# A third matmul on 128 rows instead of 64 in the up-projection of a fused attention, FFT-mixing and token-mixing kernel

## The chip, the cores and the metric

The kernel runs on 1 core of one Trainium2 chip. The metric is the device time of the whole program in microseconds, from the first to the last instruction with the launch around it, as the median of several runs. One more execution was taken with the hardware profiler; all rows of the trace come from that execution.

## What is computed

Three layers follow each other on a tensor of 4 batches, 4224 tokens and 192 features. The first is a convolution over the last 7 tokens with weights from a softmax. The second adds the real part of a two-dimensional FFT, normalizes, and applies a two-layer MLP of width 768. The third rotates by learned angles, mixes the tokens with two 4224x4224 matrices, and applies one more small dense layer. In the second layer, which the change touches:

```python
mixed = np.real(X).astype(np.float32)          # X: fft over tokens, then features
u = x + mixed
un = (u - mu) / np.sqrt(var + 1e-06)
ch = np.maximum(un @ w_ch1, 0.0) @ w_ch2       # 192 -> 768 -> 192
return (u + ch).astype(np.float32)
```

The token mixing of the third layer is `yr + yi`, with `yr = w_tok_r @ zr` and `yi = w_tok_i @ zi`; it holds by far the most arithmetic.

## The kernel before

**Precision.** TensorE is fed 32-bit words in its `F32R` form. Where more precision is wanted, an operand is split into a high part, which `F32R` holds exactly, and a low part, the rest. A product is then high x high + low x high + high x low. The weights arrive as 64-bit words, and `convert` (line 346) makes float32 of them from the bytes, on ScalarE and VectorE, and splits them into high and low parts. This byte-wise conversion is in the kernel before and after and is not touched.

**Two stages.** The prologue does the convolution and the FFT. `main_phase` then runs everything else in one interleaved program whose order is written out by hand as a list of steps: each step `t` of the last loop issues half of a slot of the token mixing, and whatever pieces of other work are due at that step.

**Token mixing.** It is cut into 33 blocks of 128 source tokens and 12 chunks of 352 target tokens. A unit is one block and one chunk; its weights are loaded by SyncE (703.6 KB each, 396 of them), converted some steps ahead (`CONV_STEPS`) into a tile `ws`, and multiplied on line 844: 128 rows, 352 columns, three products of parts. In the paired phases a slot is 12 matmuls into one PSUM tile of the pool `ps_y` (3 buffers); VectorE adds the result to `acc` (line 431).

**Preparation.** The inputs of the mixing, `z`, are made in 66 preparations `prep(k)`, one for each token block and pair of batches, on 256 columns (two batches of 128 tokens). From the fourth on, a preparation begins every `PAIR_STEPS` = 36 steps; the first four (k = 0, 2, 1, 3, in `BEGIN`) begin before the mixing does. In a preparation, step 7 transposes the normalized rows, steps 8 and 9 split them into `uT`; steps 13 to 31 (`MLP_STEPS`) hold the MLP in six pieces of 128 hidden features, each of which is `up(ft)` (five matmuls into a PSUM tile `psh`, lines 537 to 541), `act(ft)` (Relu on ScalarE at line 549, its low part on VectorE at line 550) and `down(ft)` (four matmuls, lines 563 and 564). The rest of the preparation makes the angles, sine and cosine and the products `z`, the last of them on GpSimd (line 674).

**The layout around the change.** The 192 input features are held as 128 + 64. `uT[:, 0]` is the high part of the first 128 features and `uT[:, 2]` their low part. `uT[:, 1]` holds the last 64 features twice: rows 0 to 63 are the high part (line 521), rows 64 to 127 the low part (line 526). The weights `w1s` lie in four slots, the high parts in 0 and 1, the low parts in 2 and 3; slots 1 and 3 hold the rows of the last 64 features twice, in rows 0 to 63 and again in rows 64 to 127. So the fourth matmul (slot 1 against `uT[:, 1]`, 128 rows) gives high x high and high x low at once, and the third (slot 3 against `uT[:, 1]`, 64 rows) gives low x high.

The page names a group of instructions by its line. A matmul of a shape `64*128 64x256` uses 64 rows and 128 columns of the array and moves 256 columns through it.

Of the kernel before, what the change touches and what calls it, by code (L numbers as in the profile page):

```python
# [379 lines left out]
def main_phase(tc, I, xs, mx, out, state):  # L380
    nc = tc.nc
    with ExitStack() as ctx:
# [14 lines left out]
        w1s = wt.tile([P, 4, DFF], F32R, name="w1s")  # L397
# [65 lines left out]
        def prep(k):  # L463
# [67 lines left out]
            def up(ft):  # L531
                def go():
                    uT = v["uT"]
                    c = slice(ft * P, ft * P + P)
                    ps = hs[ft] = ps_h.tile([P, 2 * P], F32, tag="h", name=f"psh{k}{ft}")
                    mm = nc.tensor.matmul
                    mm(ps, w1s[:, 0, c], uT[:, 0], start=True, stop=False)  # L537
                    mm(ps, w1s[:, 2, c], uT[:, 0], start=False, stop=False)  # L538
                    mm(ps, w1s[:64, 3, c], uT[:64, 1], start=False, stop=False)  # L539
                    mm(ps, w1s[:, 1, c], uT[:, 1], start=False, stop=False)  # L540
                    mm(ps, w1s[:, 0, c], uT[:, 2], start=False, stop=True)  # L541

                return go
# [24 lines left out]
            for ft in range(6):  # L568
                a, b, c = MLP_STEPS[ft]
# [125 lines left out]
        for i in range(HEAD):  # L695
            c, n = slots[3 * i][1], slots[3 * i][3]
# [34 lines left out]
        start = {}  # L731
# [80 lines left out]
        for t in range(T0, 2 * len(slots) + 24):  # L812
# [21 lines left out]
            js, c, m, n0 = slots[t // 2]  # L834
            pr, mo = divmod(m, 3)
            parts_n = 2 * len(js)
            if t % 2 == 0:
                ps = ps_y.tile([P, 1, TCH], F32, tag="y", name=f"y{t}")
# [127 lines left out]
```

## Time and profile before

| What | Value |
|---|---|
| Median of 3 runs | 3552.22 us (3549.4 to 3553.26) |
| The profiled execution: its time | 3549.07 us |
| The profiled execution: its span | 3547.4 us |
| TensorE matmul busy (PE) | 3397.7 us, 96% of the span, 20980 instructions |
| TensorE weight load busy (PEld) | 3248.7 us, 92% |
| VectorE busy (DVE) | 2408.4 us, 68% |
| ScalarE busy (ACT) | 2108.3 us, 59% |
| GpSimd busy (POOL) | 743.8 us, 21% |
| Mean DMA rate | 109 GB/s |

PE is the array at work on matmuls and PEld its loading of the stationary operand, which may overlap. The matmuls are pipelined, so the durations of neighbours overlap too; the distance from one start to the next is what a matmul costs in a dense stream. An arrow `<-` names what ended a wait.

### The profile page before, as it was taken

Reading aid. Unit: us, or ns where it says so; the run is one execution under the profiler, and the core shown is the slowest. Engines: PE = TensorE matmul, PEld = TensorE weight load, DVE = VectorE, ACT = ScalarE, POOL = GpSimd, SP = SyncE. Lnnn points to the kernel's source line nnn. Section 1 sums busy time; section 2 is a strip of 40 time slices with the busy share of each in tenths; the row PEclk is TensorE's granted clock in tenths of the full one; section 3 lists DMA queues with packets and bytes.
Section 4 is the critical chain, followed back from the end, with each engine's and each line's share of the span. In section 5 each row is a group of like instructions: output and inputs, shape, how many; then the busy total and the mean of one; then the engine's idle time right before and its main releaser. Section 6 shows DMA issues by size and latency. Waiting matters only on the chain.

```text
span 3547.4 us, 54487 instructions
## 1 busy us (share of the span) xinstructions
PE 3397.7 (96%) x20980; PEld 3248.7 (92%) x20980; DVE 2408.4 (68%) x5351; ACT 2108.3 (59%) x3280; POOL 743.8 (21%) x672
## 2 busy tenths in 40 slices
PE   4778799999999999999999999999999999999999
PEld 3667689999999999999999999999999999999999
DVE  8998566666666666666666666666666666666666
ACT  1333656666666666666666666666666666666643
POOL 8997111111111111111111111111111111111133
PEclk8889899999999999999999999999999999999999
DMA  4464123332323233232333323333333333333333
GB/s 158 164 207 136 60 91 100 106 105 101 108 99 107 97 105 107 99 107 99 107 101 105 108 99 107 100 106 100 103 107 100 107 100 107 104 102 107 108 121 117
DMA packets 119668, 388.03 MB, mean 109 GB/s; under 512 B 10096, under 2 KB 64112, under 8 KB 118768
## 3 DMA queue, kind: packets, MB, share of 16 engines
q1 hardware_dynamic: 116672, 376.62, 31.7%
q10 hardware_dynamic: 2736, 7.94, 0.6%
q8 instruction: 164, 2.69, 0.3%
q14 instruction: 96, 0.79, 0.1%
HBM read 351.88 MB, written 32.64 MB: 108 GB/s over the span
## 4 chain that ended last, share of the span: by engine, by line
PE 85%; ACT 1%; DVE 1%; POOL 0%; issue 0%; DMA 0%; POOLq 0%; ACTq 0%; DVEq 0%
PE y L844 63%; PE ch L563 4%; PE psh L540 3%; PE psh L539 3%; PE fy L787 2%; PE ch L564 2%; PE psh L537 1%; PE psh L541 1%; PE psh L538 1%; PE pst L621 1%; PE pst L609 1%; PE psu L513 1%; PE psx L593 0%; ACT cq L360 0%; DVE f L369 0%; ACT cq L361 0%
## 5 line engine op out<-in xcount | busy, mean ns | idle before, releaser
L844 PE MATMUL y<-ws,z 128*128 128x352 f32 x14256 | 2483.7, 325 | 7.2 <-DVE acc L433 4.4
L844 PEld LDWEIGHTS y<-ws,z 128*128 128x128 f32 x14256 | 2277.7, 189 | 9.2 <-DVE acc L433 4.9
L431 DVE TENSOR_TENSOR acc<-y,acc 128x352 f32<-128x352 f32 (+1 forms) x1158 | 597.7, 516 | 239.3 <-PE y L844 231.4
L374 ACT CAST ws<-f 128x704 fp32r<-128x704 f32 x396 | 309.1, 781 | 424.3 <-DVE f L369 424.3
L360 ACT ACTIVATE cq<-cq,bounds 128x704 uint8<-128x704 uint8 x396 | 347.6, 878 | 162.3 <-DVE cq L357 162.0
L363 DVE SCALAR_TENSOR_TENSOR cq<-cx,cq 128x176 int32<-128x176 int32 x396 | 135.5, 342 | 446.7 <-ACT cq L361 446.2
L663 POOL TENSOR_TENSOR r<-r,x 128x256 f32<-128x256 f32 (+1 forms) x260 | 188.0, 754 | 1167.7 <-ACT r L656 1167.7
L367 ACT ACTIVATE f<-cq 128x704 int32<-128x704 int8 x396 | 312.9, 790 | 135.9 <-DVE cq L363 135.8
L369 DVE SCALAR_TENSOR_TENSOR f<-raw,f 128x704 int32<-128x704 int32 x396 | 355.2, 897 | 33.8 <-ACT f L367 33.5
L376 DVE TENSOR_TENSOR ws<-f,ws 128x704 fp32r<-128x704 f32 x396 | 352.1, 889 | 30.8 <-ACT ws L374 30.6
L361 ACT ACTIVATE cq<-cq,bounds 128x704 uint8<-128x704 uint8 x396 | 349.4, 882 | 13.0
L550 DVE SCALAR_TENSOR_TENSOR g<-psh,g 128x256 fp32r<-128x256 f32 x384 | 162.0, 422 | 258.7 <-ACT g L549 258.4
L355 ACT COPY cx<-raw 128x704 uint8<-128x704 uint8 x396 | 326.1, 823 | 0.0
L496 POOL TENSOR_SCALAR rs<-mv 128x2 f32<-128x2 f32 x66 | 13.2, 200 | 1330.3 <-DVE mv L495 1301.4
L563 PE MATMUL ch<-w2s,g 128*128 128x384 f32 x768 | 241.5, 351 | 2.6 <-DVE spare L579 1.3
L549 ACT ACTIVATE g<-psh 128x256 fp32r<-128x256 f32 x384 | 144.0, 375 | 121.4 <-PE psh L541 121.4
L564 PE MATMUL ch<-w2s,g 128*128 128x192 f32 x768 | 194.1, 253 | 0.6 <-DVE g L550 0.5
L674 POOL TENSOR_TENSOR z<-r,z 128x768 fp32r<-128x768 f32 x66 | 121.9, 1847 | 135.1 <-ACT z L669 135.1
L564 PEld LDWEIGHTS ch<-w2s,g 128*128 128x128 f32 x768 | 146.7, 191 | 2.2 <-DVE g L550 2.2
L563 PEld LDWEIGHTS ch<-w2s,g 128*128 128x128 f32 x768 | 144.9, 189 | 4.1 <-ACT g L549 2.5
L149 POOL TENSOR_TENSOR pa<-pa,pb 128x768 f32<-128x768 f32 (+1 forms) x76 | 147.2, 1937 | 5.9
L540 PE MATMUL psh<-uT,w1s 128*128 128x256 f32 x384 | 148.3, 386 | 0.0
(172 smaller groups left out, 3830.3 us busy)
## 6 DMA issues: line engine op xcount, KB each, us to landing
raw<-in_W SPq DMA_DIRECT2D x396, 703.6 KB
xin<-in_xa SPq DMA_DIRECT2D x28, 960.0 KB
out<-fo SPq DMA_DIRECT2D x24, 528.0 KB
mx<-mxd SPq DMA_DIRECT2D x63, 192.0 KB
xs<-xn SPq DMA_DIRECT2D x28, 384.0 KB
mxd<-mxt SPq DMA_DIRECT2D x4, 1632.0 KB
xin<-in_xa SPq DMA_DIRECT2D x4, 1056.0 KB
wraw<-in_wts ACTq DMA_DIRECT2D x1, 3263.6 KB
```

The costliest lines, as they stand in the source:

```text
L355: nc.scalar.copy(x.bitcast(U8), tops)
L360: nc.scalar.activation(q8, q8, AF.Relu, bias=bounds[:, 0:1], scale=-1.0)
L361: nc.scalar.activation(q8, q8, AF.Relu, bias=bounds[:, 1:2], scale=-8.0)
L367: nc.scalar.activation(ti, q.bitcast(I8), AF.Copy, scale=2.0**24)
L369: nc.vector.scalar_tensor_tensor(ti, words, 5, ti, op0=ALU.logical_shift_right, op1=ALU.bitwise_or)
L374: nc.scalar.copy(h, t)
L376: nc.vector.tensor_tensor(out=l(), in0=t, in1=h.bitcast(F32), op=ALU.subtract)
L431: nc.vector.tensor_tensor(out=d, in0=v, in1=d, op=ALU.add)
L540: mm(ps, w1s[:, 1, c], uT[:, 1], start=False, stop=False)
L563: nc.tensor.matmul(ch[:, i, 0 : 2 * D], g[:, 0, t], w, start=ft == 0, stop=False)
L564: nc.tensor.matmul(ch[:, i, D : 2 * D], g[:, 1, t], w[:, :D], start=False, stop=ft == 5)
L844: nc.tensor.matmul(ps[:, 0], zz[hl], s[:, hw, ri], start=q + n == 0, stop=q == parts_n - 1 and n == 2)
```

## The change

The third of the five matmuls of `up` takes all 128 rows of its two operands instead of the first 64. Its upper 64 rows add low x low, the product of the low parts of the last 64 features, which the kernel before leaves out. The number of instructions stays, and nothing else is touched.

```diff
                     mm(ps, w1s[:, 0, c], uT[:, 0], start=True, stop=False)
                     mm(ps, w1s[:, 2, c], uT[:, 0], start=False, stop=False)
-                    mm(ps, w1s[:64, 3, c], uT[:64, 1], start=False, stop=False)
+                    mm(ps, w1s[:, 3, c], uT[:, 1], start=False, stop=False)
                     mm(ps, w1s[:, 1, c], uT[:, 1], start=False, stop=False)
                     mm(ps, w1s[:, 0, c], uT[:, 2], start=False, stop=True)
```

## Rows read from the trace of the kernel before

**Rows 1.** Busy time by stage: us, busy of PE, PEld, DVE, ACT, POOL, granted clock, DMA.
```profile
core 0: us, PE busy (x) PEld busy (x) DVE busy (x) ACT busy (x) POOL busy (x), PEclk, DMA share, GB/s
400.00:462.00 62.00, 46.29 (x253) 38.50 (x253) 37.58 (x88) 32.34 (x58) 13.65 (x19) 0.86 0.16 54
...
1000.00:2000.00 1000.00, 1000.00 (x6223) 964.15 (x6223) 656.84 (x1466) 640.55 (x959) 123.86 (x154) 1.00 0.31 104
```

**Rows 2.** Chain of work that ended last, 520 to 3320 us: shares, two pieces.
```profile
by line: PE y L844 75.8%; PE ch L563 4.8%; PE psh L540 4.1%; PE psh L539 4.1%; PE ch L564 2.3%; PE psh L537 1.5%; PE psh L541 1.5%; PE psh L538 1.5%; PE pst L621 1.4%; PE pst L609 1.2%; PE psu L513 1.0%; PE psx L593 0.5%; PE psx L594 0.2%
...
570.91 6.72 PE y L844 x42
616.87 6.72 PE y L844 x42
```

**Rows 3.** PE groups by shape, 520 to 3320 us: busy us, mean ns, idle before.
```profile
L540 PE MATMUL psh<-uT,w1s 128*128 128x256 f32 x366 | 140.7, 384 | 0.0
L539 PE MATMUL psh<-uT,w1s 64*128 64x256 f32 x366 | 139.7, 382 | 0.0
...
L537 PE MATMUL psh<-uT,w1s 128*128 128x256 f32 x366 | 102.7, 281 | 0.0
```

**Rows 4.** PE in order of time, one up piece: start us, us, instruction.
```profile
1507.00 0.28 PE L537 MATMUL psh<-uT,w1s 128*128 128x256 f32 x1
1507.12 0.28 PE L538 MATMUL psh<-uT,w1s 128*128 128x256 f32 x1
1507.33 0.38 PE L539 MATMUL psh<-uT,w1s 64*128 64x256 f32 x1
1507.64 0.38 PE L540 MATMUL psh<-uT,w1s 128*128 128x256 f32 x1
1507.86 0.28 PE L541 MATMUL psh<-uT,w1s 128*128 128x256 f32 x1
1507.98 2.09 PE L844 MATMUL y<-ws,z 128*128 128x352 f32 x12
```

**Rows 5.** Line 539 in three stretches: count, ns min/median/max, first and last start.
```profile
L539 PE MATMUL psh<-uT,w1s x12: 379/380/580, 379.0 to 419.5; 64*128 64x256 f32 x12
...
L539 PE MATMUL psh<-spare,w1s x12: 379/382/384, 394.8 to 458.2; 64*128 64x256 f32 x12
...
L539 PE MATMUL psh<-uT,w1s x6: 380/382/382, 495.7 to 513.9; 64*128 64x256 f32 x6
...
L539 PE MATMUL psh<-uT,w1s x366: 380/382/383, 539.3 to 3317.5; 64*128 64x256 f32 x183
```

**Rows 6.** Chain of work, 370 to 540 us: the last VectorE piece, first up piece.
```profile
499.88 0.35 DVE g L550
500.27 0.36 PE ch L564
...
501.42 0.12 PE psh L537
501.54 0.12 PE psh L538
```

**Rows 7.** PE's waits, 378 to 462 us: us in total, times, longest us.
```profile
PE psu L513 <- DVE spare L503: 10.0, 1, 10.0
```

**Rows 8.** PE in order of time at the lower clock, one up piece.
```profile
382.34 0.47 PE L537 MATMUL psh<-uT,w1s 128*128 128x256 f32 x1
...
383.85 0.42 PE L541 MATMUL psh<-uT,w1s 128*128 128x256 f32 x1
384.06 0.52 PE L563 MATMUL ch<-w2s,g 128*128 128x384 f32 x1
```

**Rows 9.** VectorE and PE in order of time around one MLP piece.
```profile
1501.45 0.42 DVE L527 TENSOR_TENSOR uT<-psu,uT 128x256 fp32r<-128x256 f32 x1
...
1508.10 0.42 DVE L550 SCALAR_TENSOR_TENSOR g<-psh,g 128x256 fp32r<-128x256 f32 x1
...
1510.08 0.25 PE L564 MATMUL ch<-w2s,g 128*128 128x192 f32 x1
```

## The prediction, made before the changed kernel was run

> **What bounds the kernel now.** I read the busy times by stage first. From 520 to 3320 us TensorE is busy for all of every stage; the row of 1000 to 2000 us stands for them, with PE at 1000.00 of 1000 us, VectorE at 656.84, ScalarE at 640.55, and a granted clock of 1.00, which is the upper of the two levels, 2.4 GHz [rows 1]. Busy is not the same as well used, so the next view is the chain of work that ended last. In that stretch it consists of TensorE's lines alone, no other engine stands in it, and it repeats: the run of 42 mixing matmuls begins at 570.91 and again at 616.87, so one preparation takes 45.96 us [rows 2]. The groups by shape say the same: no idle time before any of them [rows 3]. So a nanosecond taken from TensorE's stream in this stretch is a nanosecond off the end, until another engine is late.
>
> The same chain shows the odd thing. The five matmuls of an up piece are alike but for one's row count, yet lines 537, 538 and 541 take 1.5% of the stretch each, and 539 and 540 take 4.1% each [rows 2]. Line 539 is the one on 64 rows; 540 follows it and has the full 128 rows, as 537 has, but its mean is 384 ns against 281 [rows 3].
>
> **What the change removes.** Starts in order of time give the cost [rows 4]: from 537 to 538 it is 0.12 us, then 0.21 to 539, 0.31 to 540, 0.22 to 541, and 0.12 to the next mixing matmul. Together the piece takes 1507.98 - 1507.00 = 0.98 us. Two plain steps of this shape are 0.12 each at the precision of the rows. The shares give a third figure: 1.5% of 2800 us over 366 pieces is 0.115 us. I take 0.117 us. Five of these are 0.585, so the piece has 0.98 - 0.585 = 0.39 us that its columns don't explain: 0.09 before the 64-row matmul starts, 0.19 between it and its follower, 0.10 after the follower. All of it lies around the passage from 128 rows to 64 and back: the weight load for the next shape isn't hidden behind the matmul of the last one. The shares check the sum: (4.1 - 1.5) x 2 = 5.2% of 2800 us is 146 us over 366 pieces, 0.40 each.
>
> With the change all five have one shape, 128 rows and 256 columns, the shape of 537 and 538. The third's own streaming costs nothing more for its rows if the 0.12 us of 537, with 128 rows, holds for it too; the trace has no plain 64-row stream beside it in this stage, so I bound that step below by 0.115 and above by 0.21, its present distance, and take 0.117, since the shape after the change is exactly that of 537.
>
> The Trainium skill has a rule that speaks against a gain: "TensorE: Matmul & The Clock Gate", in "Why this matters for your kernels", says that a matmul on 32 contraction rows takes the same time as one on 128. By it alone the third matmul costs the same on 64 rows as on 128 and nothing is won, which is a rival below; the rows of lines 539 and 537, 382 against 281 ns on equal columns, disagree with it for a 64-row matmul in this place [rows 3]. "TensorEngine Tiling (Array Packing)", under "Key Properties", says that a change of the tiling mode drains the engine. By that both passages of each piece cost time and both go, and the sum stays what the rows give.
>
> **How often, and where.** There are 396 pieces, 66 preparations of six [rows 5]. 366 lie from 539.3 to 3317.5 us, wholly in TensorE's stretch. The six of the fifth preparation start their third matmul between 495.7 and 513.9; the chain passes from VectorE to TensorE at 500.27 and holds the up piece at 501.42 [rows 6], so four of these count. That makes 370 x 0.39 = 144 us.
>
> The other 26, from 379.0 to about 500 us, lie where the clock is granted at 0.86 on average and PE is busy 46.29 of 62 us [rows 1], and where TensorE waits 10.0 us at one point for VectorE's work on the normalized rows [rows 7]. If that wait swallows all, they give nothing; if all is passed on they give 26 x 0.39 = 10 us, plus about one for the few pieces at the lower clock. I take 4, under the middle, as the long wait lies behind most of them.
>
> **What it adds.** No instruction, no DMA, no semaphore of a new kind; the queues of SyncE and GpSimd are passed by nothing. The third matmul now also reads rows 64 to 127 of `uT[:, 1]`, which line 526 on VectorE writes just ahead of 527. The fourth read them already, 0.31 us later. In the preparation of the rows, 527 ends at 1501.87 and a first up piece starts at about 1504, some 2 us later [rows 9], so the earlier read waits for nothing; without that cover it could cost at most those 0.31 us in one piece of six, some 20 us in all. The upper rows of the weight slot are filled long before, by the same conversion as the lower.
>
> **What is late next.** A preparation shrinks by 6 x 0.39 = 2.36 to 43.6 us. VectorE's 656.84 us in 1000 are 30.2 us of 45.96, or 69% of 43.6, and ScalarE's 640.55 become 68%, so neither is the bound on the mean [rows 1]. In the dense part of the MLP, VectorE's low part (line 550) ends at 1508.52 and its reader on TensorE starts at 1510.08, a cover of 1.56 us [rows 9]. Two up pieces lie ahead of that reader and bring it 0.78 us nearer; half of the cover stays. Behind 550 on VectorE's queue is the next addition to `acc`, which frees one of three `y` buffers. If each preparation lost another 0.5 us there, it would be 30 us.
>
> **The sum.** The profiled execution took 3549.07 us, a span of 3547.4 and 1.7 around it, 3.15 us below the median of the runs. 3549.07 - 144 - 4 = 3401; on the median, 3552.22 - 148 = 3404 us.
>
> **The rivals.**
> - *Only half of the passage goes.* If the delay after the fourth matmul (0.10 us to 541) belongs to its operands and not to the row change, 370 x 0.10 = 37 us stay: 3441 us. For it: the fourth and the third share `uT[:, 1]`. Against: 541 after 540 has the shapes of 538 after 537, which start 0.12 us apart [rows 4].
> - *Another engine takes the bound in the MLP part*, VectorE through its low parts and `acc`. With the 0.5 us above: 3434 us; at 1 us, 3465. Against it stand the 69% and the cover that is left.
> - *No gain*, the rule of the skill: the distances belong to the third and fourth place in the sum, or row count costs nothing either way: 3552 us. Against it stand 539 and 540 beside 537 [rows 3].
> - *Slower: the clock.* The array works on more rows, and the lower clock level is granted during the up pieces. At the lower level a plain step was 0.21 us (383.85 to 384.06) and a whole piece before the change 1.72 [rows 8]. A changed piece would take 5 x 0.21 = 1.05 us against 0.98 now, +0.07: 370 times that is +26 us, 3578 us. It decides from the point where over 0.39 / (1.05 - 0.585), some 84%, of the pieces run at the lower level. Against it: four of the five matmuls and all of the mixing have 128 rows already, at a granted clock of 1.00 [rows 1, 4].
>
> That the change doesn't do what it says would be this: the compiled instruction keeps 64 rows. Its price is that of no gain, and it is in that chance.
>
> **How the numbers follow.** Full gain 0.85; half of the passage 0.04; another engine late 0.06; no gain 0.03; slower 0.02. The forecast's own bounds are 3392 (all 26 early pieces pass on their 11 us, and a few us of spread between runs) and 3412 (none do, and the piece falls short by some 0.01 us). Toward the other cases I reach to 3425, part of the way to a late VectorE. A difference of 0.2%, about 7 us, is what a measurement of this kernel can tell from none. Faster by more than that: 0.95; within it 0.03; slower 0.02.
>
> **What would show it.** In the profile after, lines 537 to 541 should each be 128*128 with about 281 ns, start 0.12 us apart, with the piece at 0.59 us; the pieces of the chain repeat every 43.6 us; the shares of 539 and 540 fall to about 1.6%; PE stays without idle time from 520 us on, and the end moves by what PE's stream lost. A later start of 541 alone would be the first rival; idle time before 564 or 844 with VectorE as its releaser the second. The forecast is wrong if line 539 on 128 rows still starts 0.2 us after 538.

## The result, and the profile after

| | Before | After |
|---|---|---|
| Median of 4 runs | 3552.74 us | 3408.51 us (3405.7 to 3410.29) |
| Ratio to before | | 0.9601, 95% interval 0.959 to 0.9613 |
| Profiled execution: time (span) | 3549.07 us (3547.4) | 3409.65 us (3407.9) |

The medians lie 144.2 us apart, the two profiled executions 139.4. The forecast was 148 us less, 3404 us, with 3392 to 3425 as its range.

The first view of the kernel after is its busy time by stage, with the columns of [rows 1]. TensorE still has no free moment in the steady stretch, at the same granted clock of 1.00; VectorE's share grew from 656.84 to 690.14 us in 1000 because the same work is done in less time.

```profile
1000.00:2000.00 1000.00, 1000.00 (x6550) 998.64 (x6550) 690.14 (x1548) 672.59 (x1009) 130.25 (x161) 1.00 0.33 109
```

The chain of work of the kernel after, from 520 to 3180 us, answers to [rows 2]. Lines 539 and 540 fell from 4.1% to 1.6%, the share that 537, 538 and 541 have too. The run of 42 mixing matmuls comes back after 611.23 - 567.55 = 43.68 us, where it was 45.96.

```profile
by line: PE y L844 79.8%; PE ch L563 5.1%; PE ch L564 2.5%; PE psh L540 1.6%; PE psh L539 1.6%; PE psh L541 1.6%; PE psh L537 1.6%; PE psh L538 1.6%; PE pst L621 1.5%; PE pst L609 1.2%; PE psu L513 1.0%; PE psx L593 0.5%; PE psx L594 0.3%
...
567.55 6.72 PE y L844 x42
611.23 6.72 PE y L844 x42
```

The groups by shape from 520 to 3180 us answer to [rows 3]: the third matmul now shows 128 rows, and its mean and the fourth's, which the change doesn't touch, are within 3 ns of the first's.

```profile
L539 PE MATMUL psh<-uT,w1s 128*128 128x256 f32 x366 | 103.5, 283 | 0.0
L540 PE MATMUL psh<-uT,w1s 128*128 128x256 f32 x366 | 103.5, 283 | 0.0
...
L537 PE MATMUL psh<-uT,w1s 128*128 128x256 f32 x366 | 102.7, 280 | 0.0
```

In order of time, one piece of the same preparation as in [rows 4] and [rows 9], with the low part on VectorE and its reader:

```profile
1457.66 0.28 PE L537 MATMUL psh<-uT,w1s 128*128 128x256 f32 x1
...
1457.78 0.28 PE L538 MATMUL psh<-uT,w1s 128*128 128x256 f32 x1
...
1457.90 0.28 PE L539 MATMUL psh<-uT,w1s 128*128 128x256 f32 x1
...
1458.02 0.28 PE L540 MATMUL psh<-uT,w1s 128*128 128x256 f32 x1
...
1458.14 0.28 PE L541 MATMUL psh<-uT,w1s 128*128 128x256 f32 x1
...
1458.26 2.09 PE L844 MATMUL y<-ws,z 128*128 128x352 f32 x12
...
1459.17 0.42 DVE L550 SCALAR_TENSOR_TENSOR g<-psh,g 128x256 fp32r<-128x256 f32 x1
...
1460.19 0.19 PEld L564 LDWEIGHTS ch<-w2s,g 128*128 128x128 f32 x1
1460.37 0.25 PE L564 MATMUL ch<-w2s,g 128*128 128x192 f32 x1
```

All starts are 0.12 us apart, and the piece takes 1458.26 - 1457.66 = 0.60 us instead of 0.98. VectorE's result is ready at 1459.59 and read at 1460.37: the cover went from 1.56 to 0.78 us, and TensorE shows no wait in the steady stretch. The low part is the stationary operand there, so it is the weight load of line 564 that needs it, and that starts earlier than its matmul: at 1509.91 before and 1460.19 after. Counted to the load, the cover went from 1.39 to 0.60 us. The load before:

```profile
1509.91 0.19 PEld L564 LDWEIGHTS ch<-w2s,g 128*128 128x128 f32 x1
```

### The profile page after: what moved, and what is told of

Read it like the earlier page. It is cut to its first block, busy times and chain, and to the rows that moved or that the text cites. A ratio compares the mean times of both kernels' runs of the same rounds, so it can differ in the third digit from the quotient of the medians.

```text
span 3407.9 us, 54487 instructions
## 1 busy us (share of the span) xinstructions
PE 3249.6 (95%) x20980; PEld 3201.5 (94%) x20980; DVE 2404.2 (71%) x5351; ACT 2103.6 (62%) x3280; POOL 744.3 (22%) x672
## 4 chain that ended last, share of the span: by engine, by line
PE 84%; ACT 1%; DVE 1%; POOL 0%; issue 0%; DMA 0%; POOLq 0%; ACTq 0%; DVEq 0%
PE y L844 66%; PE ch L563 4%; PE fy L787 2%; PE ch L564 2%; PE psh L540 1%; PE psh L539 1%; PE psh L541 1%; PE psh L537 1%; PE psh L538 1%; PE pst L621 1%; PE pst L609 1%; PE psu L513 1%; PE psx L593 0%; ACT cq L360 0%; DVE f L369 0%; ACT cq L361 0%
## 5 line engine op out<-in xcount | busy, mean ns | idle before, releaser
L145 POOL TENSOR_TENSOR pb<-xin,w 128x768 f32<-128x768 f32 (+1 forms) x76 | 123.2, 1620 | 0.0
```

## The experiments

The theory under test: a passage of the array from 128 rows to 64 and a passage back cost about 0.2 us each, whatever the matmul reads and wherever it stands. Its rivals: the delay belongs to the third and fourth matmul and their shared operand; each 64-row matmul is slow in itself; every departure from the neighbours' shape costs.

Each was run in rounds with the kernel before on the same chip. A first set compares with 3550.89 us before, a second with 3549.24.

**The 64 rows moved to another matmul.** The change, with the fifth on 64 rows:

```diff
-                    mm(ps, w1s[:, 0, c], uT[:, 2], start=False, stop=True)
+                    mm(ps, w1s[:64, 0, c], uT[:64, 2], start=False, stop=True)
```

> The changed kernel with its fifth matmul on 64 rows (the upper 64 rows of that product are left out); the third stays on 128. Passage theory: any 64-row matmul between 128-row ones costs one passage to 64 rows and one back, wherever it stands and whatever it reads, so the 0.385 us a piece come back: 3408.5 + 370 x 0.385 = 3551 us, with the late starts now at 541 and at the mixing matmul behind it. Operand theory: the delay belonged to the third and fourth, which share uT[:, 1]; the fifth reads another tile part, so 3408 us.

It took 3548.59 us, 0.9995 of before (0.9985 to 1.0005): the whole gain is gone again. Its PE in order of time:

```profile
1507.35 0.28 PE L540 MATMUL psh<-uT,w1s 128*128 128x256 f32 x1
1507.56 0.38 PE L541 MATMUL psh<-uT,w1s 64*128 64x256 f32 x1
1507.87 0.43 PE L844 MATMUL y<-ws,z 128*128 128x352 f32 x1
```

The steps of 0.21 and 0.31 us moved along, to the fifth and to the mixing matmul behind it, which has another operand, another shape and another PSUM tile. The operand theory falls. The forecast's first rival, a delay of the fourth's own operands, falls with it.

**96 rows.** The kernel before, with

```diff
-                    mm(ps, w1s[:64, 3, c], uT[:64, 1], start=False, stop=False)
+                    mm(ps, w1s[:96, 3, c], uT[:96, 1], start=False, stop=False)
```

> The kernel before with its third matmul on 96 rows instead of 64 (32 of the low x low rows are in). If only the passage to the 64-row setting of the array costs, 96 rows run in the 128-row setting and the time is that of the change, 3408 us, with 540 starting 0.12 us after 539. If any row count other than that of the neighbours costs, 3552 us.

It took 3407.74 us, 0.96 of before (0.9585 to 0.9614), the time of the change. Its PE in order of time:

```profile
1502.32 0.28 PE L539 MATMUL psh<-uT,w1s 96*128 96x256 f32 x1
1502.44 0.28 PE L540 MATMUL psh<-uT,w1s 128*128 128x256 f32 x1
```

So it isn't a row count other than the neighbours' that costs: 96 rows run among 128 at 0.12 us a step.

**32 rows.** The same line with `w1s[:32, 3, c], uT[:32, 1]`.

> The kernel before with its third matmul on 32 rows instead of 64 (the other 32 rows of that product are left out). Passage theory: a 32-row setting is another division of the array, and there and back cost the same, 3551 us. If the delay goes by the number of rows (fewer to load and to fill), 3480 us or another time clear of 3551.

3551.61 us, 1.0006 of before (0.9997 to 1.0015). The steps are those of 64 rows, though half as many rows are loaded and multiplied:

```profile
1508.13 0.38 PE L539 MATMUL psh<-uT,w1s 32*128 32x256 f32 x1
1508.44 0.39 PE L540 MATMUL psh<-uT,w1s 128*128 128x256 f32 x1
1508.66 0.28 PE L541 MATMUL psh<-uT,w1s 128*128 128x256 f32 x1
```

**64 columns instead of 64 rows.** The changed kernel, with

```diff
-                    mm(ps, w1s[:, 3, c], uT[:, 1], start=False, stop=False)
+                    mm(ps[:64], w1s[:, 3, ft * P : ft * P + 64], uT[:, 1], start=False, stop=False)
```

> The changed kernel with its third matmul on 128 rows but only 64 stationary columns (the third product is left out for half of the hidden features). If every change in how the array is divided costs a passage, columns as well as rows, 3551 us. If only the rows matter, 3408 us or a little less.

3401.59 us, 0.9582 of before (0.9568 to 0.9596). No passage is seen on either side:

```profile
1509.47 0.28 PE L538 MATMUL psh<-uT,w1s 128*128 128x256 f32 x1
1509.59 0.28 PE L539 MATMUL psh<-uT,w1s 128*64 128x256 f32 x1
1509.71 0.28 PE L540 MATMUL psh<-uT,w1s 128*128 128x256 f32 x1
```

By the medians, this kernel took 6.9 us less than the change. Its third weight load takes 135 ns instead of 188, and its steady stretch, from the first to the last start of line 539, is 3170.4 - 535.7 = 2634.7 us against 2639.6 after the change; how the one leads to the other wasn't tried.

**Two 64-row matmuls, apart and together.** The first kernel is the one before, with its fifth matmul on 64 rows as well, so that the 128-row fourth stands between two of 64:

> The kernel before with a second 64-row matmul, the fifth, so that third and fifth stand on 64 rows with the 128-row fourth between them (the upper 64 rows of the fifth's product are left out). Two passages there and two back in each piece. Passage theory: 3551 + 370 x 0.385 = 3693 us. If the later matmuls hide part of a second passage, between 3600 and 3693. If what costs is one fixed pause per piece: 3551 us.

The second puts the same fifth ahead of the fourth, so that the two of 64 rows are neighbours:

```diff
-                    mm(ps, w1s[:, 1, c], uT[:, 1], start=False, stop=False)
-                    mm(ps, w1s[:, 0, c], uT[:, 2], start=False, stop=True)
+                    mm(ps, w1s[:64, 0, c], uT[:64, 2], start=False, stop=False)
+                    mm(ps, w1s[:, 1, c], uT[:, 1], start=False, stop=True)
```

> The same two 64-row matmuls as in the run with two passages there and back, but next to each other: the fifth's product goes ahead of the fourth's (the same 64 rows of one product are left out). One passage there and one back. Passage theory: 3551 us, as with one 64-row matmul, and the second 64-row matmul starts about 0.12 us after the first. If each 64-row matmul is itself slow, 3551 + 370 x 0.19 to 370 x 0.385 = 3621 to 3693 us.

Apart they took 3706.14 us, 1.0441 of before (1.0425 to 1.0457); together 3550.65 us, 1.0004 (0.9995 to 1.0013). The same five matmuls, in another order, differ by 155 us. So a 64-row matmul isn't slow in itself, and the passages are what is paid for. The chains of the two, in the same view as above, give the price: a preparation takes 48.32 us apart and 45.98 together.

```profile
731.24 6.72 PE y L844 x42
779.56 6.72 PE y L844 x42
```
```profile
709.50 6.72 PE y L844 x42
755.48 6.72 PE y L844 x42
```

Against the 45.96 us of before, the second pair of passages costs (48.32 - 45.96) / 6 = 0.39 us a piece, as much as the first. The time missed the theory's 3693 us by 13, and that lies ahead of the steady stretch. The third matmul starts first at 378.7 us and opens the steady stretch at 552.3, where before it was 379.0 and 539.3 [rows 5]; from 378 to 420 us the granted clock was 0.59, between its two levels, against 0.88 before. The theory's 370 pieces left 26 early ones out. The stage before, and with the two 64-row matmuls apart (columns as in [rows 1]):

```profile
378.00:420.00 42.00, 38.71 (x193) 30.36 (x192) 24.12 (x74) 20.49 (x54) 5.86 (x9) 0.88 0.26 88
```
```profile
378.00:420.00 42.00, 41.94 (x137) 31.35 (x135) 18.57 (x59) 13.16 (x39) 1.77 (x4) 0.59 0.24 82
```

One part of what I expected of the neighbours was a miss: the second was to start 0.12 us after the first, and it took 0.22:

```profile
1505.26 0.28 PE L538 MATMUL psh<-uT,w1s 128*128 128x256 f32 x1
1505.47 0.39 PE L539 MATMUL psh<-uT,w1s 64*128 64x256 f32 x1
1505.69 0.28 PE L540 MATMUL psh<-uT,w1s 64*128 64x256 f32 x1
1505.90 0.39 PE L541 MATMUL psh<-uT,w1s 128*128 128x256 f32 x1
1506.12 0.33 PE L844 MATMUL y<-ws,z 128*128 128x352 f32 x1
```

The piece still takes 1506.12 - 1505.14 = 0.98 us; its first matmul starts at 1505.14. The rows read best so: a passage delays two starts in a row, the one that passes by about 0.09 us and the next by about 0.10. Here the four late starts stand apart, at 0.21 to 0.22 each. In the kernel before, the second delay of the way down and the first of the way back fall on the same matmul, which makes its 0.31 [rows 4].

The weight loads say more of it. First those of the kernel before, in the piece of [rows 4], then those of the two neighbours:

```profile
1507.00 0.19 PEld L538 LDWEIGHTS psh<-uT,w1s 128*128 128x128 f32 x1
1507.33 0.18 PEld L539 LDWEIGHTS psh<-uT,w1s 64*128 64x128 f32 x1
1507.64 0.19 PEld L540 LDWEIGHTS psh<-uT,w1s 128*128 128x128 f32 x1
1507.75 0.19 PEld L541 LDWEIGHTS psh<-uT,w1s 128*128 128x128 f32 x1
```
```profile
1505.47 0.18 PEld L539 LDWEIGHTS psh<-uT,w1s 64*128 64x128 f32 x1
1505.58 0.19 PEld L540 LDWEIGHTS psh<-uT,w1s 64*128 64x128 f32 x1
1505.90 0.19 PEld L541 LDWEIGHTS psh<-uT,w1s 128*128 128x128 f32 x1
```

Without a passage, a load starts some 0.11 us ahead of its matmul, while the one before still runs: line 538's at 1507.00 for 1507.12, and the neighbour's at 1505.58 for 1505.69. Across a passage it starts only with its own matmul, at 1507.33 and 1507.64, and at 1505.47 and 1505.90. In the steady stretch of every kernel here with a 64- or 32-row matmul, the third to fifth matmul's loads that cross a passage start 0 to 3 ns ahead of their matmuls, and the others 113 ns or more. With 96 rows, with 64 columns and after the change, all five have that lead.

**No third matmul.** The changed kernel with line 539 taken out:

> The changed kernel without its third matmul (low x high of the last 64 features is left out). If the third costs one plain step of 0.119 us and TensorE stays the bound, 3408.5 - 370 x 0.119 = 3364 us, and the fourth starts 0.12 us after the second. If VectorE is about to be late behind the shorter MLP part, less is won and idle time stands before 564 or 844 in the steady stretch: 3380 to 3408 us.

3364.03 us, 0.9475 of before (0.9461 to 0.9489), 44.5 us below the change: 0.12 us for each of 370. So a 128-row step of 256 columns costs its 0.12 us and no more, and the 64-row form had cost 0.12 + 0.39. VectorE is hardly late even now: between 520 and 3100 us, TensorE's only wait in this kernel is one of half a microsecond, for VectorE:

```profile
PE psx L592 <- DVE x L578: 0.5, 1, 0.5
```

**The first four preparations alone.** The kernel before, with

```diff
-                    mm(ps, w1s[:64, 3, c], uT[:64, 1], start=False, stop=False)
+                    r3 = P if k in BEGIN else 64
+                    mm(ps, w1s[:r3, 3, c], uT[:r3, 1], start=False, stop=False)
```

> The change in the first four preparations alone (24 pieces, from 379 to about 460 us), the other 62 as before. My forecast took 4 us for the early pieces, 0 to 11 as bounds: 3547 us. If the waits of that stretch swallow the gain, as the profile after suggests (the steady stretch began only about 1 us earlier): 3550 to 3551 us.

3547.43 us, 0.9993 of before (0.9984 to 1.0001): by the time alone, the 4 us and no gain can't be told apart. The trace tells more. The rows are the third matmul (here on line 540), with counts and first and last start as in [rows 5]; first this kernel, then the changed one:

```profile
L540 PE MATMUL psh<-uT,w1s x12: 278/281/415, 378.8 to 416.3; 128*128 128x256 f32 x12
...
L540 PE MATMUL psh<-uT,w1s x6: 380/382/383, 492.2 to 510.6; 64*128 64x256 f32 x6
```
```profile
L539 PE MATMUL psh<-uT,w1s x12: 278/280/415, 382.5 to 420.0; 128*128 128x256 f32 x12
...
L539 PE MATMUL psh<-uT,w1s x6: 282/282/283, 495.4 to 513.1; 128*128 128x256 f32 x6
```

From the first third matmul of all to the first of the fifth preparation it is 495.7 - 379.0 = 116.7 us before [rows 5], 492.2 - 378.8 = 113.4 here and 495.4 - 382.5 = 112.9 after the change. The early stretch became 3.3 and 3.8 us shorter. This isn't shown to be the passages alone, because the granted clock changed with them: from 378 to 420 us it was 0.88 before and 0.96 in both of these kernels. The kernel with 32 rows, which has as many passages as before, was granted 0.72 there and took 499.0 - 378.5 = 120.5 us. In the profiled execution after the change this can't be seen from the steady stretch alone, because there the stretch ahead of the pieces, in which nothing was changed, ended 3.5 us later than in that of before.

## Why the prediction was right

- **The bound.** TensorE alone sets the end from 520 us on: held. Its stream lost 3317.5 - 539.3 - (3177.7 - 538.1) = 138.6 us in the steady stretch, from the first and last start of line 539 in [rows 5] and after (538.1 to 3177.7), and the profiled execution lost 139.4.
- **The price of a piece.** The saving was right in kind and a little too large. I took 0.585 us for the piece after; it is 0.59 or 0.60. On the mean of the steady stretch, steps three to five are 0.120 us and not 0.117. The gain is 138.6 us over 365 piece-to-piece intervals, 0.380 instead of 0.39, so 370 pieces give 140.6 instead of 144.
- **Where it sits.** I put all three late starts down to the passage and its way back, against a rival that kept 0.10 us for the fourth's operands. The moved 64 rows, and the two orders of the same matmuls, showed that. The reason given, a weight load that isn't hidden behind the last matmul, is seen too: the loads across a passage start only with their own matmuls, 1507.33 and 1507.64.
- **The early pieces.** 4 us taken, 3.3 and 3.8 read from two traces. The 4 was chosen between bounds of 0 and 11, so it is luck in part, and the share of the clock in the measured figures is open. With 140.6 the sum is about 144 us, and the medians give 144.2.
- **What is late next.** Half of VectorE's cover was to stay, 0.78 us; 0.78 stayed. The reader was taken to be the matmul; it is the weight load ahead of it, so less was left than the forecast thought: 0.60 us. Idle time of TensorE in the steady stretch stayed at nothing.
- **The added reads.** No wait on `uT` was to appear in the steady stretch, and none did. The clock was to stay at its upper level, and the row by stage shows 1.00.

Of the two rules of the Trainium skill, "TensorE: Matmul & The Clock Gate" ("Why this matters for your kernels"), that fewer contraction rows don't make a matmul shorter, agrees as far as the runs go: a step took 0.12 us on 96 and on 128 rows, and 32 rows took the time of 64. No run has a step on 32 rows without a passage. The rule leaves out the passage, and that is all of this change. The other rule of the Trainium skill, "TensorEngine Tiling (Array Packing)" ("Key Properties"), that a change of the tiling mode drains the engine, agrees for 64 and 32 rows, at some 0.39 us there and back; 64 columns on 128 rows, which that page lists as a tiling mode too ("Available Configurations"), showed no such cost here.

**What stays open.** The traces show that a passage holds its weight load back to the start of its own matmul and delays two starts in a row; they don't show why the load is held, or what the array does in that time. Why the later steps of a run of five are 0.120 us rather than 0.117 wasn't tried; the weight load is busy for 998.64 of 1000 us after the change, and the shorter load of the kernel with 64 columns went with a shorter stretch, which points at the loads and doesn't show it.

## What to carry to other kernels

In a dense stream of TensorE, look at the distance between starts, and at a matmul on 64 or 32 rows between matmuls on 128 first: here it cost 0.39 us more than its 0.12, and the full row count costs nothing where the operands already hold usable rows. Where 64-row matmuls are needed, put them next to each other, since the price is for each passage and not for each matmul. The gain arrives in full only while TensorE alone is the bound: check the cover of the next engine, counted to the weight load that reads its result: here 1.39 us, of which 0.79 were taken.

## What was not expected of the hardware

- A passage delays the next two starts by about 0.09 and 0.10 us, rather than one start by the whole: the load that crosses starts with its own matmul, and the one behind it only about 0.11 us later.
- What the prediction didn't treat, and the runs settled: 96 rows run among 128 without a passage, and so do 64 columns on 128 rows; 32 rows cost as much as 64.
- In the early stretch the granted clock went with the passages: from 378 to 420 us, in the profiled execution of each kernel, it was 0.96 to 1.00 in the five whose pieces there have no passage, 0.72 to 0.92 in the four with one there and one back, and 0.59 in the one with two. No run shows why.
- The stretch ahead of the first up piece, alike in all these kernels, ended several microseconds apart: the first third matmul is at 379.0 us before and at 382.5 after. One profiled execution is therefore no measure of a few microseconds at the end.
